# Queries by seven products in a third pass, with their exponentials kept in memory

## The chip, the cores and the metric

The kernel runs on one core of one Trainium2 chip. The core has five engines that run side by side, each with its own list of instructions: TensorE (PE; its weight loads are listed as PEld) multiplies matrices and writes to PSUM; VectorE (DVE), ScalarE (ACT) and GpSimd (POOL) work on elements; SyncE (SP) here only issues DMA transfers. The metric is device time in microseconds for one execution, as the median over runs.

## The reference

S is 2048 rows of x, D is 1024, there are H = 32 heads of DH = 32, and the hidden width FF is 3584. All is float32.

```python
xn = _layernorm(x)
q, k, v = split(xn @ wqkv)                       # [32 heads, 2048, 32] each
pq = einsum("bhsd,hdf->bhsf", q, w_phi); pk = einsum("bhsd,hdf->bhsf", k, w_phi)
phi_q = concat([softmax(pq), softmax(-pq)])      # the same for phi_k
kv = einsum("bhsf,bhsd->bhfd", phi_k, v);  z = einsum("bhsf->bhf", phi_k)
o = einsum("bhqf,bhfd->bhqd", phi_q, kv) / (einsum("bhqf,bhf->bhq", phi_q, z) + 1e-6)
s = o.reshape(S, D) @ wo
g = silu((silu(xn @ w1) * (xn @ w3)) @ w2)
out = x + s * g
```

So there are two branches on the same normalised x: linear attention with a feature map of two softmaxes per head, and a gated feed-forward network. The output joins them.

## The kernel before

**Numbers.** Every large product is made of float32r matmuls. An operand is split into a rounded high part and a low rest (`split`, L89: a copy on ScalarE and a subtraction on VectorE), and a product of two operands takes three matmuls, high by high, high by low and low by high (`PASSES`, L87).

**Seven products.** Most of the large products use a seven-product scheme for 2x2 blocks in place of eight: two tiles of 128 rows form a pair (`pairs`, L66), each operand has seven combinations of its four blocks (`ANAMES`, `BNAMES`, in the order of `ORDER`, L60), and the seven products accumulate in three PSUM banks, from which the four output blocks are read at given points. A pair costs 7 x 12 = 84 matmuls of 128x512 where the plain form costs 96 for the same two outputs of 512 columns.

**Stages, in order.**

1. The start: x is loaded, normalised and transposed; w_phi is folded into the key and query weights (`fold`, L243), so that pk and pq come directly from xn. Transposed x is also written to memory (`store_x`, L223, tensor `xn_d`).
2. Feed-forward products with w1 and w3 (loop at L545), in two halves `tb` of 28 steps `f`, each of seven products: 196 "side steps" per half. Beside them run side tasks at steps given by hand (`at`, `room`, `store_quad`, L383 to L408): the x operands of the second half (`side_x`), weight folds (`side_fold`), the seven combinations of the key and value weights for two passes (`side_kv`, eight units), in the second half those of w2 (`side_w2`) and the splits of query and output weights (`side_split`). Their results go to memory (`wkv_d`, `wqo_d`, `wo_d`, `w2_d`). `room` spreads the splits by an allowance of VectorE time per step. In this stage the instructions of all engines, SyncE too, are in the order of the program text (`in_order`, L46).
3. Keys and values (loop at L763): two passes `c`, each over eight pairs. Each pass has its own seven weight operands of 2 MB in slots `big0` to `big6` and two spare slots (`HOMES`, L148); the next pass's operands are fetched into slots as they come free in the last pair (`fetch`, L157). The x operands of each pair are loaded again (`reload`, L535). In a pair (`heads`, L649) the key half goes through `features` (L104: largest and smallest per head, two differences, exponential, sum) and `scaled`, and small products `kv` (L639) add phi_k by v into one bank `pkv`. `kv_out` (L694) writes the sums with sixteen small stores, for the first pass in the first pair of the second, and for the second pass in step r = 1 of the next stage (L924).
4. The feed-forward product with w2 (loop at L901): seven blocks `kb` times eight pairs, again by seven products, summed over kb in SBUF tiles `acc`. The hidden values are loaded (`hr`) and split per step. In the last kb, `gate` (L819) applies silu to finished sums and stores them (`g_d`), query weights are loaded into the freed tiles, and the queries of tile 0 are computed.
5. The last stage (loop at L1005): for each of sixteen tiles of 128 rows the queries are projected by plain products (`project_q`, L868: 24 matmuls for each of two halves `c` of 512 columns), `queries` (L838) makes the exponentials and scales them, `attend` (L973) transposes them and multiplies by the key/value sums `kvu`, and `finish` (L993) projects by wo (another 48 matmuls), multiplies by the gate, adds x and stores.

Outside the parts that are in program order, the order of each engine's instructions comes from a planner that estimates when each could run. Tiles come from pools with a fixed number of buffers per tag; a new tile waits for the release of an old one.

In `queries` the sum with z is folded in: `ez` is the exponentials times `zb` (the key sums, the same for every row), made by GpSimd, and VectorE's sums of e and ez give one factor per head and sign:

```python
nc.gpsimd.tensor_mul(ez, ef, zb[c])
nc.vector.tensor_reduce(sums[:, 0]..., e3, axis=AX.X, op=OP.add)
...
nc.vector.tensor_mul(e3, e3, by...to_broadcast([P, H, DH]))
```

## Time and profile before

| | |
|---|---|
| median of 3 runs | 2473.88 us (2471.05 to 2474.21) |
| the profiled execution | 2476.03 us, span 2474.2 us |
| TensorE busy | 2408.9 us, 97% |
| VectorE busy | 1718.2 us, 69% |
| ScalarE busy | 896.9 us, 36% |
| GpSimd busy | 668.5 us, 27% |
| DMA | 521.02 MB, mean 211 GB/s |

In the profiled execution stage 3 begins at about 1180 us, stage 4 at about 1514, and the last stage at about 2068. In a row of the profile, "L100 PE MATMUL pm<-wq,xh" is line 100 of the kernel, the engine, the operation, and the tiles written and read by their names; after "x" stands the count, then the busy time and the mean duration of one in nanoseconds, then the engine's idle time before these instructions and what ended it. A row of the timeline begins with its start and its duration. SPq is SyncE's queue of DMA issues.

### The profile page before, as it was taken

The page shows a single profiled execution, that of the slowest core. Times are in us where ns is not written, and L with a number is a line of the kernel's source. Part 1 is how long each engine was busy: PE and PEld are TensorE (multiplying, and loading weights), DVE is VectorE, ACT ScalarE, POOL GpSimd, SP SyncE. Part 2 cuts the span into 40 slices and gives each one's busy share as a digit, 9 for nine tenths or more (in the row PEclk, how much of TensorE's full clock was granted, in tenths as well). Part 3 has the DMA queues.
Part 4 walks back from the last instruction along what each step waited for, and adds up shares of the span by engine and source line. Part 5 has one row for each costly group of instructions (what it writes and reads, how often), then busy time and mean ns, then how long its engine had stood idle before and what let it go on. Part 6 is the DMA issues. An engine that isn't in the chain of part 4 may idle for free.

```text
span 2474.2 us, 35921 instructions
## 1 busy us (share of the span) xinstructions
PE 2408.9 (97%) x13648; PEld 1969.3 (80%) x13648; DVE 1718.2 (69%) x2573; ACT 896.9 (36%) x1555; POOL 668.5 (27%) x481
## 2 busy tenths in 40 slices
PE   5999999999999999999999999999999999999999
PEld 4788878888778888888788788788888887777777
DVE  8667678774477777774566655587888877777775
ACT  6544544443345454443111113422222243222221
POOL 1233445443344545541000000011111112232222
PEclk9999999999999999999999999999999999999999
DMA  8667788875877777766967763623444376322222
GB/s 294 206 218 229 251 275 307 289 261 178 261 276 273 273 264 267 259 227 253 356 213 294 268 209 123 224 98 145 179 170 179 108 275 232 96 73 90 78 85 69
DMA packets 300812, 521.02 MB, mean 211 GB/s; under 512 B 24544, under 2 KB 172000, under 8 KB 298848
## 3 DMA queue, kind: packets, MB, share of 16 engines
q1 hardware_dynamic: 300640, 518.74, 61.1%
q8 instruction: 107, 1.75, 0.3%
q14 instruction: 65, 0.53, 0.1%
HBM read 331.22 MB, written 187.44 MB: 210 GB/s over the span
## 4 chain that ended last, share of the span: by engine, by line
PE 81%; DMA 8%; DVE 5%; issue 2%; ACT 2%; SPq 1%; POOL 1%; ACTq 0%; DVEq 0%; POOLq 0%
PE bankb L575 18%; PE pm L100 14%; PE bankb L882 12%; PE bankc L575 8%; PE bankb L659 7%; PE bankc L882 6%; PE banka L575 4%; PE bankc L659 3%; PE banka L882 3%; PE banka L659 2%; DVE bo L92 1%; PE po L986 1%; PE pkv L644 1%; DMA wkv_d1T<-wkvo 1%; PE pt L980 1%
## 5 line engine op out<-in xcount | busy, mean ns | idle before, releaser
L92 DVE TENSOR_TENSOR bo<-rw,bo 128x512 fp32r<-128x512 f32 x336 | 292.6, 872 | 129.8 <-ACT bo L91 126.3
L91 ACT CAST bo<-rw 128x512 fp32r<-128x512 f32 x336 | 206.4, 622 | 69.8 <-DMA w_d5T<-w2o 8.7
L882 PE MATMUL bankb<-bo,as 128*128 128x512 f32 x816 | 202.3, 391 | 5.2 <-DVE acc L894 5.2
L892 POOL TENSOR_TENSOR acc<-acc,u 128x512 f32<-128x512 f32 x48 | 62.7, 1307 | 483.4 <-ACT u L891 383.0
L270 POOL TENSOR_TENSOR rw<-rw,t 128x512 f32<-128x512 f32 x56 | 79.2, 1414 | 404.5 <-DVE bo L92 404.4
L100 PE MATMUL pm<-wq,xh 128*128 128x512 f32 x768 | 185.3, 394 | 0.0
L882 PEld LDWEIGHTS bankb<-bo,as 128*128 128x128 f32 x816 | 153.9, 189 | 37.7 <-DVE acc L894 5.7
L575 PE MATMUL bankb<-op0A,bo 128*128 128x512 f32 x672 | 160.3, 392 | 8.1 <-ACT bo L91 4.5
L575 PE MATMUL bankb<-op1A,bo 128*128 128x512 f32 x672 | 159.8, 394 | 7.7 <-DVE u L603 4.6
L100 PEld LDWEIGHTS pm<-wq,xh 128*128 128x128 f32 x768 | 142.0, 188 | 31.4 <-issue 2.8
L575 PE MATMUL bankb<-op0S,bo 128*128 128x512 f32 x672 | 163.7, 392 | 2.3 <-ACT h L588 1.3
L575 PE MATMUL bankc<-op0S,bo 128*128 128x512 f32 x672 | 164.3, 393 | 1.2 <-ACT u L601 1.2
L575 PE MATMUL bankb<-op1S,bo 128*128 128x512 f32 x672 | 161.7, 389 | 2.2 <-ACT u L594 2.2
L575 PE MATMUL bankc<-op1S,bo 128*128 128x512 f32 x672 | 161.7, 389 | 0.8 <-issue 0.8
L575 PEld LDWEIGHTS bankb<-op1A,bo 128*128 128x128 f32 x672 | 126.6, 189 | 37.3 <-DVE u L603 7.5
L575 PEld LDWEIGHTS bankb<-op0A,bo 128*128 128x128 f32 x672 | 125.3, 188 | 37.6 <-DVE u L603 5.9
L575 PEld LDWEIGHTS bankb<-op1S,bo 128*128 128x128 f32 x672 | 126.0, 188 | 29.0 <-ACT u L594 2.9
L575 PEld LDWEIGHTS bankc<-op0S,bo 128*128 128x128 f32 x672 | 126.5, 189 | 28.0 <-ACT u L601 1.6
L575 PEld LDWEIGHTS bankc<-op1S,bo 128*128 128x128 f32 x672 | 126.0, 188 | 27.6 <-issue 1.2
L575 PEld LDWEIGHTS bankb<-op0S,bo 128*128 128x128 f32 x672 | 124.8, 188 | 28.7 <-ACT u L594 1.9
L882 PE MATMUL bankc<-bo,as 128*128 128x512 f32 x576 | 147.2, 391 | 0.0
L100 PE MATMUL pm<-wos,oT 128*128 128x512 f32 x576 | 136.3, 390 | 0.0
(201 smaller groups left out, 4679.9 us busy)
## 6 DMA issues: line engine op xcount, KB each, us to landing
rw<-in_w SPq DMA_DIRECT2D x112, 512.0 KB, 5.2
h_d<-h SPq DMA_DIRECT2D x112, 256.0 KB, 7.0
hr<-h_d SPq DMA_DIRECT2D x56, 512.0 KB, 3.5
xoS<-xo_d0S SPq DMA_DIRECT2D x32, 512.0 KB, 9.8
xoS<-xo_d1S SPq DMA_DIRECT2D x32, 512.0 KB, 3.9
room<-in_w SPq DMA_DIRECT2D x56, 256.0 KB, 6.4
xoA<-xo_d0A SPq DMA_DIRECT2D x24, 512.0 KB, 9.4
xoA<-xo_d1A SPq DMA_DIRECT2D x24, 512.0 KB, 4.0
```

The lines of the kernel that those rows point to most:

```text
L91: nc.scalar.copy(hi, src)
L92: (by or nc.vector).tensor_sub(lo, src, hi.bitcast(F))
L100: nc.tensor.matmul(p, xT[dch][:, a], w(dch, b), start=n == 0, stop=n == 3 * ND - 1)
L270: nc.gpsimd.tensor_sub(b11, b22, t2)
L575: nc.tensor.matmul(bank[b], bo[bn][:, w, k], ao[an][:, u, k], start=first and n == 0, stop=LAST[b] == an and n == 11, skip_group_check=True)
L644: nc.tensor.matmul(pkv[sl, m], e[:, m // 4, (m % 4) * P + 32 * h:(m % 4) * P + 32 * h + 32], v[:, 4 * (m % 4) + h], start=first and m == 0 ...
L659: nc.tensor.matmul(bank[b], xo[an][:, u, k], wb[bn][:, w, k], start=an in ("A11", "A12", "S1") and n == 0, stop=LAST[b] == an and n == 11, ...
L882: nc.tensor.matmul(bank[b], t[:, u, pos + k], bos[kb, bn, k][:, w], start=first and n == 0, stop=LAST[b] == an and n == 5, skip_group_chec ...
L892: nc.gpsimd.tensor_add(c, c, u)
L980: nc.tensor.transpose(pt[:, g, :], e[:, (4 * q + g) * P:(4 * q + g + 1) * P], ident)
L986: nc.tensor.matmul(po[32 * g:32 * g + 32, hh, q * P:(q + 1) * P], kvu[sl, G * c + 4 * q + g], et[sl, g], start=True, stop=True, skip_group ...
```

## The change

The queries move from the last stage into stage 3 as a third pass, with c = 2, over the eight pairs, by seven products like the keys. The loop around the seven products is now a function of its own, `seven`, used by `heads` and by the new `queries`. The query weights are no longer split and stored as `wqo_d`; three side units more (`side_kv` with c = 2, one of four in the first half, three in the second) make their seven combinations. The third pass makes the exponentials (`spikes`) and stores them (`e_d`); the last stage loads them (`load_e`), makes the sums and scales (`scales`, for both halves at once, one of the two scalings on GpSimd), two tiles ahead of their use. The transposed x is not stored any more. The splits of wo move from the second feed-forward half into the first two passes of stage 3. The sixteen stores of the second pass's key/value sums move from stage 4 into the first pair of the third pass. In the last stage `attend` of tile i + 1 is cut into parts that stand between groups of twelve matmuls of tile i's output projection. `kvu` is loaded earlier. Side tasks get new steps (folds every 6 in place of 14, key/value units every 11 in place of 12, the units of the second half every 9.5).

```diff
-    HOMES = [(4, 5, 6, 0, 1, 3, 2), (7, 8, 4, 5, 6, 0, 1), (2, 3, 7, 8, 4, 5, 6), (0, 1, 2, 3, 4, 5, 6)]
+    HOMES = [(4, 5, 6, 0, 1, 3, 2), (7, 8, 4, 5, 6, 0, 1), (2, 3, 7, 8, 4, 5, 6), (0, 1, 2, 3, 7, 8, 4),
+             (5, 6, 0, 1, 2, 3, 4)]
...
+    def spikes(t, c, p, e):
+        mm = small.tile([P, 2, 16], F, name="mm2")
+        p3 = p.rearrange("p (h f) -> p h f", f=DH)
+        nc.vector.tensor_reduce(mm[:, 0, :], p3, axis=AX.X, op=OP.max)
+        nc.vector.tensor_reduce(mm[:, 1, :], p3, axis=AX.X, op=OP.min)
+        e4 = e.rearrange("p (h s f) -> p h s f", s=2, f=DH)
+        nc.vector.tensor_sub(e4[:, :, 0], p3, mm[:, 0, :].unsqueeze(2).to_broadcast([P, 16, DH]))
+        nc.vector.tensor_sub(e4[:, :, 1], mm[:, 1, :].unsqueeze(2).to_broadcast([P, 16, DH]), p3)
+        nc.scalar.activation(e, e, AF.Exp)
+        nc.sync.dma_start(e_d[t][c], e)
+
+    def queries(i, xo, wb, steps, pend):
+        t0, t1 = pairs[i]
+        for an, pb in seven(xo, wb):
+            if an == "A11":
+                k0 = work.tile([P, 512], F, name="k0", tag="w")
+                nc.scalar.copy(k0, pb)
+            elif an == "A12":
+                nc.vector.tensor_add(k0, pb, k0)
+                e01 = rwp.tile([P, 2, 1024], F, name="eq", tag="rw")
+                spikes(t0, 0, k0, e01[:, 0])
+            elif an == "S2":
+                d0 = work.tile([P, 512], F, name="d0", tag="w")
+                nc.scalar.copy(d0, pb)
+            elif an == "S1":
+                if pend:
+                    kv(*pend)
+                    kv_out(1, pkv)
+                d1 = work.tile([P, 512], F, name="d1", tag="w")
+                nc.scalar.copy(d1, pb)
+            elif an == "S3":
+                nc.vector.tensor_add(d1, pb, d1)
+                spikes(t1, 1, d1, e01[:, 1])
+            elif an == "S4":
+                nc.vector.tensor_add(d0, pb, d0)
+                e10 = rwp.tile([P, 2, 1024], F, name="eq", tag="rw")
+                spikes(t0, 1, d0, e10[:, 0])
+            else:
+                spikes(t1, 0, pb, e10[:, 1])
+            next(steps)
+        return None
...
-    for c in range(2):
+    for c in range(3):
...
+                    if c < 2:
+                        split_wo(c, i, j)
...
+                    if end and c < 2:
+                        if j < 4 or (j == 4 and c == 0):
+                            wbn.update(fetch(c + 3, j + 2))
+                        if j == 6 and c == 1:
+                            wbn.update(fetch(c + 3, 6))
...
-            pend = heads(i, xo, wb, steps(), pend)
+            pend = (queries if c == 2 else heads)(i, xo, wb, steps(), pend)
...
+    def scales(e):
+        sums = small.tile([P, 2, 2, 16, 2], F, name="sums")
+        for c in range(2):
+            ez = accp.tile([P, 1024], F, name="ez", tag="accE", bufs=3)
+            nc.gpsimd.tensor_mul(ez, e[c], zb[c])
+            nc.vector.tensor_reduce(sums[:, 0, c]..., e[c]..., axis=AX.X, op=OP.add)
+            nc.vector.tensor_reduce(sums[:, 1, c]..., ez..., axis=AX.X, op=OP.add)
+        ...
+        for c, eng in enumerate((nc.vector, nc.gpsimd)):
+            e3 = e[c].rearrange("p (h f) -> p h f", f=DH)
+            eng.tensor_mul(e3, e3, by[:, c]...to_broadcast([P, H, DH]))
+        return e
...
-            kv(*pend)
-            kv_out(1, pkv)
             late_rw += [rwp.tile([P, 2, 2, 512], R, name="late", tag="rw") for _ in range(2)]
...
+    for oT in halves(es[0]):
+        pass
+    for i in range(NT):
+        out_i = output(i, oT)
+        if i + 3 < NT:
+            es[i + 3] = load_e(i + 3)
+        if i + 2 < NT:
+            scales(es[i + 2])
         if i + 1 < NT:
-            xT = split_q(xf)
-        e1 = queries(p, 1)
-        finish(pend[0], oT)
-        pend = (i, e0, e1)
+            for oT in halves(es[i + 1]):
+                next(out_i)
+        for _ in out_i:
+            pass
```

`halves` runs `attend` for both halves of a tile in four parts; `output` is the former `finish`, which now stops after every twelve matmuls to let the next part in.

238 lines of the change are left out of this document (106 added, 132 removed).

## The prediction

> **What bounds the kernel now.** I read the page's busy shares and its chain first, then the chain in order of time and TensorE's instructions at the places where the change cuts, then the stages' busy times, the queue of SyncE, and the DMA answers for the key and value stage.
>
> ```profile
> span 2474.2 us, 35921 instructions
> PE 2408.9 (97%) x13648; PEld 1969.3 (80%) x13648; DVE 1718.2 (69%) x2573; ACT 896.9 (36%) x1555; POOL 668.5 (27%) x481
> PE 81%; DMA 8%; DVE 5%; issue 2%; ACT 2%; SPq 1%; POOL 1%; ACTq 0%; DVEq 0%; POOLq 0%
> ```
>
> TensorE is busy for 97% of the span and carries 81% of the chain. A busy TensorE need not be TensorE at its rate, so the next rows give the rate.
>
> ```profile
> 2041.09 5.60 PE L100 MATMUL pm<-wq,xh 128*128 128x512 f32 x24
> 2046.53 1.52 PE L882 MATMUL bankc<-bo,as 128*128 128x512 f32 x6
> ```
>
> The 24 matmuls of one query projection begin at 2041.09 and the next work begins at 2046.53: 5.44 us, or 0.2267 us each.
>
> ```profile
> 1409.69 2.94 PE bankb L659 x12
> 1430.57 2.94 PE bankb L659 x12
> 2310.99 20.43 PE pm L100 x89
> 2336.64 20.43 PE pm L100 x89
> ```
>
> In the chain in order of time, a pair of key/value tiles takes 1430.57 - 1409.69 = 20.88 us: 84 matmuls are 84 x 0.2267 = 19.04, the rest is the small products of `kv`. A tile of the last stage takes 2336.64 - 2310.99 = 25.65 us: 96 large matmuls are 21.77, and 3.88 are left for `attend`. In the chain both repeat evenly on TensorE alone, so its own work sets their length. Stage by stage (busy us of each engine; clock, DMA share and GB/s last):
>
> ```profile
> 20.00:40.00 20.00, 16.52 (x112) 14.29 (x110) 19.07 (x45) 14.07 (x29) 2.59 (x2) 1.00 0.83 265
> 1540.00:1560.00 20.00, 14.76 (x55) 11.52 (x54) 7.30 (x16) 6.86 (x14) 0.00 (x0) 0.83 0.74 237
> 2040.00:2084.00 44.00, 41.54 (x249) 33.56 (x247) 30.69 (x54) 20.11 (x22) 8.49 (x4) 1.00 0.80 285
> ```
>
> TensorE's idle microseconds gather at the start and at seams such as 1540-1560 and 2040-2084; the rest is dense.
>
> **1. The query product itself.** Removed: 16 tiles x 2 halves x 24 = 768 large matmuls. Added: 8 pairs x 7 products x 12 = 672. The difference is 96, and the trace shows the rate: 96 x 0.2267 = **-21.8 us**. The bounds are narrow, because the added matmuls have the shape and the loop of the two existing passes (19.04 per pair). The new pass so costs 8 x 19.04 = 152.3 us and the last stage falls to 25.65 - 48 x 0.2267 = 14.77 us a tile. This holds as far as the other engines keep up in both places.
>
> **2. VectorE and ScalarE in the new pass.** Per pair there are four `spikes` and three additions, with the durations of the same operations today:
>
> ```profile
> L844 DVE TENSOR_REDUCE mm<-pm 128x16 f32<-128x512 f32 x32 | 22.0, 688 | 35.3 <-PE pm L100 35.3
> L894 DVE TENSOR_TENSOR acc<-bankb,acc 128x512 f32<-128x512 f32 x152 | 104.3, 686 | 24.9 <-PE bankb L882 18.8 <-ACT as L91 2.0
> L850 ACT ACTIVATE e<-e 128x1024 f32<-128x1024 f32 x32 | 34.0, 1062 | 105.0 <-DVE e L847 105.0
> L855 DVE TENSOR_REDUCE sums<-e 128x32 f32<-128x1024 f32 x32 | 39.0, 1219 | 24.0 <-ACT e L850 24.0
> L851 POOL TENSOR_TENSOR ez<-e,zb 128x1024 f32<-128x1024 f32 x32 | 76.7, 2395 | 219.7 <-issue 133.4 <-ACT e L850 86.3
> L1001 POOL TENSOR_TENSOR gx<-gx 128x512 f32<-128x512 f32 x30 | 38.9, 1298 | 71.1 <-issue 37.5 <-DVE rho L858 29.3 <-DVE gx L1000 4.4
> ```
>
> VectorE: four passes over the bank each (two reductions, two differences, all at about the 0.688 of the first row), 16 x 0.688 + 3 x 0.686 = 13.1 us; ScalarE, four exponentials of 1.062 and three copies, about 6. Both lie under the 19.04 of TensorE: nothing. The exponential buffers are two, and the first of a pair is written again one pair later: its second store is issued about 5 us after the fifth product, and 10.9 us lie between that product and the next write, so the store may take 6 us to land. If it is late, VectorE waits, with 6 us to spare.
>
> **3. DMA in the new pass.** Per pair: seven reloaded operands of 512 KB (3.67 MB), four stores of exponentials (2.10 MB), and in pairs 1 to 4 two blocks of w2 operands (1.05 MB), 6.82 MB at most. At 19.04 us that asks for 358 GB/s.
>
> ```profile
> DMA packets 669, 8.49 MB, mean 425 GB/s; under 512 B 70, under 2 KB 70, under 8 KB 177
> 1380.00:1400.00 20.00, 20.00 (x166) 16.13 (x168) 12.85 (x18) 3.66 (x5) 0.21 (x2) 1.00 0.95 368
> ```
>
> The first line is the DMA answer for 1340 to 1360, where the operands of the second pass are fetched: 425 GB/s held for 20 us. The second row gives 368 GB/s at a share of 0.95, with TensorE busy for all of its 20 us. The demand is 84% of that, so I take no cost for the steady pass. The Trainium skill, "DMA: Bandwidth & Descriptors", section "Where 436 GB/s comes from", says that for transfers between HBM and SBUF the HBM side binds at about 358 GB/s; by it pairs 1 to 4 would have nothing to spare, and what is carried over from the seam would lengthen the pass by about 5 us, an estimate worked out below. This trace does not agree: it shows 425.
>
> **4. The new seam between pass two and pass three.** Five operands of 2 MB are fetched as their slots come free, and the sixteen tiny stores of the key/value sums follow on the same queue. Today's seam between pass one and two shows both:
>
> ```profile
> 1346.04 3.01 PE L659 MATMUL bankb<-op3B,xoA 128*128 128x512 f32 x12
> ...
> 1361.26 0.32 SPq L704 DMA_DIRECT2D kv_d<-kva  x1
> ...
> 1375.07 0.81 SPq L540 DMA_DIRECT2D xoA<-xo_d0A  x2
> xoS<-xo_d0S SPq DMA_DIRECT2D x4, 512.0 KB, 18.3
> 1388.74 1.43 PE L659 MATMUL bankb<-op3B,xoA 128*128 128x512 f32 x5
> ```
>
> SyncE spends 13 us or more on the sixteen stores, and only at 1375.07 are the operands loaded for the pair that begins at 1388.74. The four loads of the fifth line, issued in the thick of it, took 18.3 us to land; a load at half of that had about 4 us to spare. In pass three two pairs and one `kv` last 38.8 us, not the 42.7 from 1346.04 to 1388.74, so the spare time is about zero, and four stores of exponentials stand in the same queue. From below, nothing; from above, one late burst, 18.3 less the 13.7 us from 1375.07 to 1388.74, about 5. I take **+2**.
>
> The seam between pass one and two gets its operands earlier (slots 7 and 8 are used too) but shares DMA with the splitting of wo: 0.79 MB a pair beside 3.67, and one subtraction and one copy of 128x512 a pair, 0.7 us each at most on engines that have 6 us to spare. Nothing.
>
> **5. The seam into the second feed-forward stage.** The last `kv` and its sixteen stores leave step 1 of that stage.
>
> ```profile
> 1529.09 0.32 SPq L704 DMA_DIRECT2D kv_d<-kva  x1
> ...
> 1541.79 0.38 SPq L736 DMA_DIRECT2D hr<-h_d  x1
> ...
> 1550.69 0.43 DVE L741 TENSOR_TENSOR sm<-hr 128x256 f32<-128x256 f32 x1 [11.44 <-DMA hr<-h_d]
> 1551.77 2.93 PE L882 MATMUL bankb<-bo,as 128*128 128x512 f32 x6 [5.24 <-DVE acc L894]
> ```
>
> The stores hold SyncE from 1529.09, the load of `hr` goes out only at 1541.79, VectorE waits 11.44 us for it, and TensorE 5.24 us for VectorE. The clock then falls (0.83 over 1540 to 1560): 55 matmuls in 20 us are 12.5 us of work, 7.5 lost. With the stores gone the whole 7.5 can come back; what is late next are the last pair's four stores of exponentials, of which the last follows its product by 4 x 0.688 + 1.062 = 3.8 us, or about 5 with the queue, and stands before the next `hr`. From 0 to -7.5; the removed queue is 12.7 us, the new hold 5, so I take **-6**.
>
> **6. The last stage.** Per tile VectorE keeps four sums and one scaling of 128x1024 at 1.219 each, six small steps of 0.17 to 0.25 (half as many as now, on twice the heads; I take 1.2 together), and the two splits and two products that today's tile has, at the 0.686 of L894: 6.1 + 1.2 + 2.74 = 10.0 us. GpSimd takes over one scaling. No GpSimd operation with a repeated factor is in the trace; the nearest row is the 2.395 of L851, and the other end twice that. So 3 x 2.395 + 2 x 1.298 = 9.8 us, at most 12.2. Both are under 14.77. But the two disturb each other:
>
> ```profile
> 2274.07 1.31 POOL L1001 TENSOR_TENSOR gx<-gx 128x512 f32<-128x512 f32 x1 [2.09 <-DVE rho L858]
> 2274.26 1.15 DVE L862 TENSOR_TENSOR rho<-rho,sums 128x16 f32<-128x16 f32 x1
> ...
> 2289.64 0.17 DVE L862 TENSOR_TENSOR rho<-rho,sums 128x16 f32<-128x16 f32 x1
> ```
>
> The same small step takes 0.17 us alone and 1.15 when it starts under a GpSimd addition, ending with it. VectorE has five operations with two operands in SBUF per tile, and GpSimd will be busy for two thirds of it, so a blocked wait is 5 x 0.66 x half of 2.4 = 4 us if they fall at random: 14.0 of 14.77, still under. Tiles are scaled two ahead, so a short wait harms nobody. For waits that do reach TensorE I take **+2**, between 0 and the case C below. The Trainium skill, "SBUF — State Buffer", section "Who interferes with whom", has the rule behind such a row: a VectorE operation with two SBUF inputs and a GpSimd operation exclude each other for a whole instruction. The trace agrees (0.17 against 1.15). By it the port is taken for at most 9.8 + 2 us of 14.77.
>
> At the head of this stage the first tile's `attend` has no projection to hide under any more. Today 2.46 us are idle between 2040 and 2084, most of it for `kvu`, which is now fetched earlier; after the change TensorE stands, but for the transposes, behind two gates of about 1.06 (as L850, the same shape on ScalarE), two copies of about half of that, and one split (as much again and 0.69): 3 to 4 us. **+1**, between -2 and +3. The end (last product, two VectorE steps, last store) stays.
>
> **7. The start.** The stores of the normalised x leave SyncE.
>
> ```profile
> 37.70 4.93 DMA xn_d<-xf
> ...
> 42.66 0.69 DVE L232 TENSOR_TENSOR xf<-xf 128x512 f32<-128x512 f32 x1 [1.01 <-DMA xn_d<-xf]
> ```
>
> One of them is in the chain, because x is then overwritten in place, but VectorE waits only 1.01 us for it and is itself busy for 19.07 of 20 us there: **-1**, between 0 and -4.9. In the first feed-forward half, ten splits of query weights go and seven of the new operands come; in the second, 22 splits go and 21 come, and the memory moved is nearly the same: nothing.
>
> Sum: -21.8 + 2 - 6 + 2 + 1 - 1 = **-23.8 us**. The profiled execution took 2476.03 us (span 2474.2), 2.15 above the median of the runs; against that median of 2473.88 the forecast is 2450.
>
> **The rivals.** *A*, the sum: 2450, with its own range 2442 to 2458 from the ends of steps 4 to 7. *B*, the third pass is fed too slowly: if SyncE's queue is held by stores that wait for exponentials, or the rate is only the 368 GB/s of the row above, every fetch after the seam is late. The pass moves 8 x 5.77 + 4 x 1.05 = 50.4 MB and carries about 6 MB over from the seam (5 x 2.10 + 3.67 + 0.79 asked for in the last pair, less 20.88 us at 425 GB/s); at 368 GB/s that is 153.3 us, 1 more than TensorE's 152.3. With the seam at its upper end (3 more) and step 5 without gain (6 more) the time is 2460. Against it speaks the 425 GB/s row. By the limit that the Trainium skill states ("DMA: Bandwidth & Descriptors", the section named in step 3) the 56.4 MB would take 157.5 us, and B would be 2464.
>
> *C*, on the other side: in the last stage the chain from GpSimd's products to VectorE's sums, to the scaling on GpSimd, becomes the beat. It decides where a tile takes more than 14.77 + 23.8/16 = 16.3 us. VectorE's 10.0 plus a wait for all of GpSimd's 9.8 would be 19.8; with the scaling on GpSimd at double price (12.2) and three fifths of it waited for, a tile takes 17.3, which is 16 x 2.5 = 40 us more: 2490. For it speaks the 1.15 row; against it, that VectorE's operations with two operands in SBUF are about 2 of its 10 us. At 15.5 a tile it would eat only half of the gain. *D*, all seams at their good ends: -21.8 - 7.5 - 2 - 1 = -32.3, so 2441. That the change does not do what it says isn't to be seen: the matmul counts are in the loops.
>
> **How the numbers follow.** A 0.58, B 0.12, C 0.16, D 0.14. A change under 0.2%, 5 us, is about what cannot be told from none here. Faster takes A and D, half of B and a fifth of C: 0.81. Same takes a sixth of B and a quarter of C, 0.06; slower the rest of both, 0.13 (a B that is worse than its price included). The range reaches from D's value to halfway between B and no change, 2440 to 2470; beyond it I leave 0.05 below and 0.15 above.
>
> **What would show it.** Right: 8 pairs of about 19.0 us after the second pass with no DMA wait above 2 us; tiles of 14.5 to 15 us in the last stage; no 5 us wait of TensorE at the start of the second feed-forward stage. Wrong: TensorE waiting for `xo` or third-pass operands, VectorE idle for `ez` while a bank waits for it, tiles above 16 us, or TensorE idle for over 6 us at the head of the last stage.

## The result, and the profile after

The changed kernel takes 2485.15 us (median of 4 runs, 2483.98 to 2485.47) where the kernel before takes 2472.47 beside it (4 runs, 2470.83 to 2474.21). The ratio is 1.005 (95% interval 1.0033 to 1.0068): it is slower by half a per cent, and not faster by one as forecast. The page of the kernel after begins:

```profile
span 2483.1 us, 35840 instructions
PE 2388.2 (96%) x13552; PEld 1950.1 (79%) x13552; DVE 1704.0 (69%) x2465; ACT 900.8 (36%) x1564; POOL 735.4 (30%) x513
```

TensorE has the 96 matmuls less that the change was to save (13552 for 13648), and 20.7 us less of busy time, yet the span has grown by 8.9 us. What came in is idle time. To see where, the span is cut where each stage's matmuls begin (one matmul of the second feed-forward stage stands 9 us ahead of its cut in the kernel after, among the last products of the third pass). These are rows of TensorE's timeline (start, duration), first of the kernel before, then of the kernel after:

```profile
1175.63 2.66 PE L659 MATMUL bankb<-op2B,xoA 128*128 128x512 f32 x11
...
1514.01 1.65 PE L882 MATMUL bankb<-bo,af 128*128 128x512 f32 x6
...
2067.72 5.61 PE L100 MATMUL pm<-wq,xh 128*128 128x512 f32 x24
```

```profile
1184.05 2.20 PE L639 MATMUL bankb<-op2B,xoA 128*128 128x512 f32 x9
...
1523.07 3.00 PE L639 MATMUL bankb<-op4B,xoA 128*128 128x512 f32 x12
...
1686.34 1.30 PE L913 MATMUL bankb<-bo,af 128*128 128x512 f32 x5
...
2233.32 1.53 PE L1002 MATMUL pt<-ident,e 128*128 128x128 f32 x12 [0.79 <-DVE acc L925]
```

| stretch | before, us | after, us | change | forecast |
|---|---|---|---|---|
| to the first pass | 1175.6 | 1184.1 | +8.4 | -1 |
| first and second pass | 338.4 | 339.0 | +0.6 | 0 |
| third pass | - | 163.3 | +163.3 | +154.3 (152.3 + 2) |
| second feed-forward stage | 553.7 | 547.0 | -6.7 | -16.9 (-10.9 of query matmuls, -6) |
| last stage, to the span's end | 406.5 | 249.8 | -156.7 | -160.2 (-163.2 of query matmuls, +2, +1) |
| sum | 2474.2 | 2483.1 | +8.9 | -23.8 |

The miss of 32.7 us has four places: 9.4 ahead of the first pass, 9.6 in the passes, 10.2 in the second feed-forward stage and 3.5 in the last one. Each has its own view. (The first pass of the same code begins up to 5 us apart from profile to profile, as said below, so the first of the four is the least certain.)

**Ahead of the first pass.** Rows of ScalarE's, VectorE's and TensorE's timelines, in order of time; the bracket tells how long the engine was idle before, and what ended it:

```profile
1083.35 0.62 ACT L90 CAST w2o<-room 128x512 fp32r<-128x512 f32 x1 [3.04 <-DMA w_d6B<-w2o]
1084.00 1.32 DVE L91 TENSOR_TENSOR w2o<-room,w2o 128x512 fp32r<-128x512 f32 x1 [2.87 <-ACT w2o L90]
1085.24 0.68 DVE L584 TENSOR_TENSOR u<-bankb,u 128x512 f32<-128x512 f32 x1
1085.98 5.76 PE L556 MATMUL bankb<-op1A,bo 128*128 128x512 f32 x24 [1.37 <-DVE u L584]
```

A split (`store_quad`) waits 3.04 us until an earlier block's store has left its buffer; VectorE's half of the split waits with it; the addition that frees a bank stands behind in VectorE's queue; TensorE waits 1.37 us for that bank.

**The seam between the second and the third pass.** SyncE's issues, and the first matmul of the third pair:

```profile
1542.15 0.32 SPq L735 DMA_DIRECT2D kv_d<-kva  x1
...
1557.86 0.30 SPq L736 DMA_DIRECT2D z_d<-zs  x1
...
1561.83 1.18 SPq L521 DMA_DIRECT2D xoA<-xo_d0A  x2
...
1569.65 4.64 PE L639 MATMUL bankb<-op4B,xoA 128*128 128x512 f32 x12 [6.61 <-DMA xoA<-xo_d0A]
```

The sixteen small stores take 16 us of the queue (the first seven 1.2 us each, most of the others about 0.5), the reloads for the third pair are issued after them, and TensorE waits 6.61 us for the first one. By stretches of 10 us (busy time of each engine; clock, DMA share and GB/s last):

```profile
1530.00:1540.00 10.00, 10.00 (x106) 8.11 (x105) 4.33 (x10) 2.51 (x4) 0.00 (x0) 1.00 1.00 422
1540.00:1550.00 10.00, 9.57 (x43) 7.62 (x42) 7.09 (x12) 3.67 (x4) 0.00 (x0) 1.00 0.89 339
1550.00:1560.00 10.00, 10.00 (x46) 8.29 (x45) 3.49 (x6) 1.17 (x2) 0.00 (x0) 1.00 0.15 23
1560.00:1570.00 10.00, 3.40 (x15) 2.57 (x14) 4.60 (x8) 2.11 (x2) 0.00 (x0) 0.82 1.03 251
```

DMA falls from 422 to 23 GB/s while the stores go out: from 1550 to 1560 the DMA engines are busy for a share of 0.15 only, with no large transfer issued between 1540.93 and 1558.85. Around the wait the granted clock is 0.82.

**The end of the second feed-forward stage.** TensorE's timeline, and GpSimd's first product with `zb`:

```profile
2200.12 2.73 POOL L884 TENSOR_TENSOR ez<-e,zb 128x1024 f32<-128x1024 f32 x1 [7.47 <-ACT acc L866]
...
2216.02 1.65 PE L913 MATMUL bankc<-late,as 128*128 128x512 f32 x6 [2.93 <-DVE acc L925]
...
2225.12 1.66 PE L913 MATMUL bankb<-late,as 128*128 128x512 f32 x6 [1.87 <-DVE acc L925]
```

```profile
2210.00:2220.00 10.00, 6.05 (x24) 4.35 (x24) 10.00 (x10) 1.53 (x2) 8.61 (x4) 1.00 0.75 254
2220.00:2233.00 13.00, 7.99 (x30) 5.32 (x30) 12.87 (x18) 3.18 (x3) 3.83 (x3) 1.00 0.77 291
```

VectorE is busy for 22.87 of 23 us: the scaling of the first two tiles stands between the additions that free TensorE's banks. Before, 48 query matmuls filled this stretch. Some of the 22.87 us is blocking inside VectorE's operations, as the same small step shows, first under a GpSimd product (2212.97 to 2215.32), then beside none:

```profile
2213.61 1.75 DVE L896 TENSOR_TENSOR by<-by,rho 128x32 f32<-128x32 f32 x1
...
2226.91 0.18 DVE L896 TENSOR_TENSOR by<-by,rho 128x32 f32<-128x32 f32 x1
```

Five operations of the scalings in this stretch (1.81, 1.75, 0.62, 2.55 and 2.61 us) take 9.3 us together; undisturbed, at 0.18 for each of the three small steps and 1.22 for each of the two scalings, they would take 3.0. So about 6 us of the stretch is of this kind, an estimate from these rows.

**The last stage.** A tile takes 15.25 us in the middle. GpSimd's timeline over one tile, and TensorE's longest wait of the stage:

```profile
2329.32 2.38 POOL L884 TENSOR_TENSOR ez<-e,zb 128x1024 f32<-128x1024 f32 x1
2333.64 1.29 POOL L1027 TENSOR_TENSOR gx<-gx 128x512 f32<-128x512 f32 x1 [1.93 <-DVE gx L1026]
2334.88 2.41 POOL L884 TENSOR_TENSOR ez<-e,zb 128x1024 f32<-128x1024 f32 x1
2339.43 1.29 POOL L1027 TENSOR_TENSOR gx<-gx 128x512 f32<-128x512 f32 x1 [2.14 <-DVE gx L1026]
2341.77 2.86 POOL L899 TENSOR_TENSOR e<-e,by 128x1024 f32<-128x1024 f32 x1 [1.06 <-DVE by L896]
2344.60 2.38 POOL L884 TENSOR_TENSOR ez<-e,zb 128x1024 f32<-128x1024 f32 x1
```

```profile
2283.52 1.11 PE L1011 MATMUL po<-et,kvu 64*32 64x128 f32 x32 [6.92 <-DVE oT L91]
```

GpSimd is idle three times per tile, each time for VectorE (1.93 + 2.14 + 1.06 = 5.1 us), and VectorE for GpSimd's `ez` in between (2.43 and 1.55 us ahead of its sums of `ez`). Neither is full; the hand-overs make a ring of 15.25 us. Ahead of the wait of 6.92 us, two small steps of the scaling (0.18 us elsewhere) took 1.90 and 2.26 us under GpSimd's products and stood before the split that TensorE waited for.

### The profile page after: what moved, and what is told of

It is laid out like the page before. It is cut to its first block, busy times and chain, and to the rows that moved or that the text cites. A ratio compares the mean times of both kernels' runs of the same rounds, so it can differ in the third digit from the quotient of the medians.

```text
span 2483.1 us, 35840 instructions
## 1 busy us (share of the span) xinstructions
PE 2388.2 (96%) x13552; PEld 1950.1 (79%) x13552; DVE 1704.0 (69%) x2465; ACT 900.8 (36%) x1564; POOL 735.4 (30%) x513
## 3 DMA queue, kind: packets, MB, share of 16 engines
q8 instruction: 107, 1.75, 0.3%
## 5 line engine op out<-in xcount | busy, mean ns | idle before, releaser
L99 PE MATMUL pm<-wos,oT 128*128 128x512 f32 x768 | 192.1, 400 | 0.0
L99 PEld LDWEIGHTS pm<-wos,oT 128*128 128x128 f32 x768 | 140.3, 189 | 33.1 <-issue 6.3
L556 PE MATMUL bankc<-op0S,bo 128*128 128x512 f32 x672 | 163.3, 391 | 2.2 <-ACT u L582 1.4
L556 PE MATMUL bankb<-op0S,bo 128*128 128x512 f32 x672 | 163.3, 392 | 2.2 <-ACT u L575 2.2
L556 PEld LDWEIGHTS bankb<-op1A,bo 128*128 128x128 f32 x672 | 126.3, 189 | 44.2 <-DVE u L584 14.3
L913 PEld LDWEIGHTS bankc<-bo,as 128*128 128x128 f32 x576 | 107.9, 188 | 24.6 <-DMA bo<-w_d0B 2.0
```

The source lines that it names most:

```text
L99: nc.tensor.matmul(p, xT[dch][:, a], w(dch, b), start=n == 0, stop=n == 3 * ND - 1)
L556: nc.tensor.matmul(bank[b], bo[bn][:, w, k], ao[an][:, u, k], start=first and n == 0, stop=LAST[b] == an and n == 11, skip_group_check=True)
L913: nc.tensor.matmul(bank[b], t[:, u, pos + k], bos[kb, bn, k][:, w], start=first and n == 0, stop=LAST[b] == an and n == 5, skip_group_chec ...
```

## The experiments

All edits are to the kernel after, but for one. Stage lengths are taken at the same cuts as above. Where the stage's code is the same as in the kernel after, the first pass began between 1179.8 and 1185.0 us in eleven profiles, with 553.3 to 556.2 us for the second half of the first feed-forward stage; the second and third pass together took 330.8 to 336.9 us in eight, the third alone 160.6 to 163.7; the second feed-forward stage took 546.5 to 548.2 in eight: less than that is no difference here.

**1. Small stores spread over the next products.**

```diff
-                    kv_out(1, pkv)
+                    kv_out(1, pkv, "h1", late_out)
...
+                    if c == 2 and i and late_out:
+                        nc.sync.dma_start(*late_out.pop(0))
...
```

> The sixteen small stores of the key/value sums, issued in one block inside the first pair of the third pass, are issued one behind each product of the pairs that follow. Theory Q (order of SyncE's queue): the reload of the second pair's operands stood behind the stores, and the DMA engines were nearly idle meanwhile (39 and 14 GB/s in 1548 to 1558); now the reload goes out some 15 us earlier, the wait of 6.61 us for xoA vanishes with the slow clock behind it, and the third pass takes 153 to 156 us instead of 163.3, the whole kernel about 2476. Rival M (memory): the 14 MB asked for around the seam are what is late, so the wait moves or stays, and the pass takes 160 us or more, with the DMA share at 1.0 throughout.

Measured: 2480.83 us, ratio to before 1.0033 (1.0022 to 1.0045). The wait of 6.61 us is gone, another of 1.56 stands a pair later, and the third pass takes 156.0 us, within theory Q's range and 4.6 us under the lowest of the eight profiles above. The second pass, which the edit does not touch, took 172.0 here for 168.4 (168.4 to 172.3 in seven of the eight, 175.7 in one), so both together took 328.0 for 331.7. The whole is 4 us below the kernel after, 2485.15, with overlapping intervals. The empty stretch is gone (410 and 419 GB/s from 1540 to 1560), but where the spread stores run among the large transfers the DMA engines move 217 GB/s at a share of 0.86 (1570 to 1580) and 196 at 1.07 (1590 to 1600). That is a first sign of a second cost, which 13 takes up.

**2. Both scalings on VectorE.**

```diff
-        for c, eng in enumerate((nc.vector, nc.gpsimd)):
+        for c, eng in enumerate((nc.vector, nc.vector)):
```

> In the scaling of a tile both halves are scaled by VectorE, none by GpSimd. Theory L (the two engines exclude each other): GpSimd's work per tile falls from about 10.2 to 7.4 us, VectorE's own scaling no longer collides, VectorE's load rises by about 1.2 to some 11.2 us of 14.3; the tiles in the middle take 14.3 to 14.6 us instead of 15.25, the last stage 234 to 238 us instead of 245.3, the whole kernel about 2477. Rival V (VectorE's load is what counts): the tiles stay at 15.2 us or grow to 15.5 and more, and the last stage takes 246 us or more.

Measured: 2486.31 us, ratio 1.0054 (1.0035 to 1.0073); the last stage takes 251.6 us for 249.8. Most tiles fell to 14.3 to 14.6 us, but four took 16.6 to 20.7, with waits of up to 3.3 us for `oT`. Theory L fell, and so did the hope that less work on GpSimd is enough.

**3. No scaling of the first two tiles at the end of the second feed-forward stage.**

```diff
             if i == 5:
-                scales(es[0])
                 es[1] = load_e(1)
             if i == 7:
-                scales(es[1])
                 es[2] = load_e(2)
```

> The scaling of the first two tiles, which stands in the last two steps of the second feed-forward stage, is left out (the first two tiles of the output so lack their scaling). Theory P (the scaling has lost its cover: 48 query products stood there before): the second feed-forward stage takes 535 to 539 us instead of 547.0, and TensorE is busy for over 9.5 of the 10 us of 25 to 15 us before its end. Rival W (what costs there are the gates' stores, the loads of wo and of the exponentials): the stage stays at 545 us or more.

Measured: 2475.54 us (one run); the second feed-forward stage takes 537.5 us for 547.0. In the stretch 2210 to 2220 of its profile:

```profile
2210.00:2220.00 10.00, 9.81 (x44) 7.78 (x43) 6.74 (x11) 3.66 (x4) 4.15 (x2) 1.00 0.92 342
```

TensorE is busy for 9.81 us, not 6.05. Theory P holds: these scalings, with all that they ask of VectorE and GpSimd, cost 9.5 us there.

**4. Three of the units left out of the second feed-forward half.**

```diff
-    for k in range(1, 4):
-        units.insert(3 * k, (side_kv, 2, k))
     for m, (unit, a, b) in enumerate(units):
-        unit(a, b, HALF + 5 + 19 * m // 2)
+        unit(a, b, HALF + 7 + 12 * m)
```

> The three units that prepare query operands in the second half of the first feed-forward stage are left out (the first half's query unit is stored in their places, so the queries are not the reference's), and the 18 units of w2 stand 12 steps apart again, as in the kernel before. Theory U (the units' GpSimd sums and their closer spacing cost the 6.4 us of that half): the second half, from the first product at 629 to the first pass, takes 547 to 550 us instead of 555.0. Rival N (the loss comes from elsewhere, from the buffers that wait for stores or from what is left out of the splitting of wo): it takes 553 us or more.

(The w2 units are fourteen, not eighteen as the expectation says.) Measured: 2485.37 us (one run). The second half takes 545.3 us for 555.0, more than theory U asked for; the run does not tell the missing units from the wider spacing of the others. But the first half became 10.6 us longer: there one unit's seven buffers were now each held until four stores had read them. That was not foreseen, and pointed to the buffers.

**5. The last stage in its written order, in pieces.** The scaling becomes a generator of three pieces, which stand between the pieces of the output product; all five engines keep the order of the text. The loads of the gate and of x for a tile's two halves also go out together, ahead of its products.

```diff
-    in_order(ENG.SP)
+    in_order(ENG.PE, ENG.Activation, ENG.DVE, ENG.Pool, ENG.SP)
...
-        if i + 2 < NT:
-            scales(es[i + 2])
+        sc = scaling(es[i + 2]) if i + 2 < NT else iter(())
+        next(sc, None)
         if i + 1 < NT:
             for oT in halves(es[i + 1]):
                 next(out_i)
+                next(sc, None)
...
```

> Last stage alone: the scaling of a tile is cut into three pieces, which stand between the pieces of attend and of the output product, and all five engines keep this written order, so that no piece stands ahead of the split that TensorE waits for. Theory O (the order in VectorE's and GpSimd's queues makes a ring of hand-overs of 15.25 us a tile, and a pile of two tiles' scalings ahead of one split costs 7 us at 2276 to 2283): tiles take 14.3 to 14.5 us throughout, the pile vanishes, and the last stage, from the first transposes to the last product block, takes 218 to 222 us instead of 231.3, the whole kernel about 2474. Rival L (GpSimd and VectorE exclude each other, in whatever order): tiles stay near 15.2 us and the stage at 229 us or more.

Measured: 2470.22 us, ratio 0.999 (0.998 to 0.9999). The last stage takes 235.0 us to the span's end for 249.8, 14.8 less (231.3 in the expectation is to the last block of products; 14.8 off that is 216.5, a little under the range). The stretches of 30 us that hold the long wait and the tile above, first in the kernel after, then here:

```profile
2270.00:2300.00 30.00, 23.08 (x200) 18.12 (x194) 26.31 (x34) 5.00 (x9) 19.08 (x10) 0.89 0.56 176
2330.00:2360.00 30.00, 28.24 (x236) 22.28 (x225) 21.46 (x30) 6.66 (x12) 19.75 (x11) 1.00 0.54 175
```

```profile
2270.00:2300.00 30.00, 30.00 (x264) 23.76 (x263) 21.14 (x32) 7.20 (x14) 21.60 (x12) 1.00 0.52 178
2330.00:2360.00 30.00, 30.00 (x290) 23.62 (x270) 20.52 (x31) 7.25 (x13) 21.60 (x12) 1.00 0.58 187
```

TensorE is busy throughout, with GpSimd no less busy than before, and every full tile takes 14.3 us. In the four later runs with this edit (8, 12, 14, 18) the stage takes 235.0 us too. Theory O holds: the order was the cost, not the load (the earlier loads of gate and x were not tried apart).

**6. VectorE relieved at the end of the second feed-forward stage.**

```diff
+        if t < 2:
+            nc.vector.tensor_reduce(kept[t][:, c], e..., axis=AX.X, op=OP.add)
...
-        elif an == "A11":
+        elif an == "A11" or an == "A22" and kb == NKB - 1 and i >= 3:
...
```

> Second feed-forward stage's end: the scalings stay where they are, but VectorE is relieved there. The plain sums of the first two tiles are formed in the third pass (four reductions of 1.22 us less), and in the last steps the addition of one more product of seven goes by ScalarE and GpSimd (about five additions of 0.69 less). Theory P (VectorE's load there is what TensorE waits for): 4.9 + 3.4 us less of VectorE's work make the second feed-forward stage 539 to 542 us instead of 547.0, and the third pass stays as it is. Rival B (the blocked VectorE operations under GpSimd's products are what costs, and GpSimd gets more work): 545 us or more.

Measured: 2492.22 us (one run); the stage takes 550.9 us for 547.0. Less work on VectorE and more on GpSimd, together, lost 4 us; experiment 8 has the first alone. Theory P in this form fell.

**7. The units' sums apart from the operands' own.**

```diff
-            b_sums(r[0], r[2], r[3], r[4])
+            nc.gpsimd.tensor_sub(r[2], r[3], r[2])
+        t1 = free(s0 + 3)
...
+        at(t1 + 1, lambda: nc.gpsimd.tensor_add(r[4], r[2], r[0]))
...
```

> First feed-forward stage: the two GpSimd sums with which a unit begins (key/value and w2 units alike) no longer stand at the step where they fall, but two steps in which the operands' own GpSimd sums are not, one each. Theory G (runs of four GpSimd sums hold up VectorE's subtractions, 1.77 us instead of 0.68): the second half takes 551 to 553 us instead of 555.0, the first half, to its end at 627.5 to 629, 1 to 2 us less too. Rival Q (what delays the steps is the buffers that wait for their stores): both halves stay within 0.7 us.

Measured: 2486.38 us (one run); first half to 626.7, second 556.9, the first pass at 1183.6. No difference: theory G fell.

**8. Three edits together** (1 in both passes, 5, and the reductions of 6).

```diff
-                        kv_out(0, pkv)
+                        kv_out(0, pkv, "h1", late_out)
...
+                    if i and late_out:
+                        nc.sync.dma_start(*late_out.pop(0))
...
```

> Three edits together: the small stores of the key/value sums are spread over the following products in the second and in the third pass, the last stage keeps its written order in pieces, and the plain sums of the first two tiles are formed in the third pass (without the further addition on GpSimd). If each cost was read rightly, they add up: second and third pass together 322 to 325 us instead of 331.7 (waits of about 3 and 6 us gone, and the slow clock behind them), the second feed-forward stage 542 to 545 instead of 547.0, the last stage 15 us shorter; the whole kernel 2458 to 2464, which is faster than both kernels. Rival: what is freed in one place is lost at the next (the reductions moved into the third pass make it longer, the end of the feed-forward stage stays at 547 since GpSimd's part sets it): 2466 or more.

Measured: 2469.57 us, ratio 0.9986 (0.9975 to 0.9996), not more than experiment 5 alone. The last stage kept its gain. The second feed-forward stage took 548.8: moving 4.9 us of reductions away bought nothing. And the passes took 331.4 together, the third one 162.3, with a new wait of 4.8 us for a reload two pairs later: what spreading gained in experiment 1 is lost here. Which of the two additions to the passes does that, the spread in the second pass or the reductions in the third, was not tried apart. The rival held.

**9. Three units without their GpSimd sums.**

```diff
+            t2.append(r[0] if plain else block())
+            if not plain:
+                b_sums(r[0], r[2], r[3], t2[0])
...
```

> The three query units in the second half of the first feed-forward stage keep their loads, copies, subtractions and stores, but form none of their four sums on GpSimd (the operands so hold plain weights, and the queries are not the reference's). Theory G (GpSimd's sums make the units dear: 12 sums of 1.3 us that block VectorE): the second half takes 549 to 552 us instead of 555.0. Rival R (the 21 copies on ScalarE and subtractions on VectorE and their buffers): 554 us or more. Between the two, both.

Measured: 2481.96 us (one run); the second half takes 553.7 us for 555.0, which is inside the spread of the same code. The sums cost nothing that can be seen: what three units and the closer spacing cost (9.7, experiment 4) is then in the splits, their buffers and their stores.

**10. Stores one step sooner in the first feed-forward stage.**

```diff
-            at(step + 2, lambda: nc.sync.dma_start(d, t.bitcast(F)))
+            at(step + 1, lambda: nc.sync.dma_start(d, t.bitcast(F)))
```

> First feed-forward stage: each prepared block is stored one step (2.7 us) after it was split, not two, so its buffer comes free one step sooner. Theory Q (ScalarE waits for a buffer that its store has not left, VectorE's next addition comes late, TensorE waits for its bank): second half 551 to 553 us instead of 555.0, first half, to its end at 627.5 to 629, 1 to 2 us less. Rival N (those waits are not what TensorE's waits hang on): both stay within 0.7 us, or SyncE waits for the split and it gets worse.

Measured: 2470.48 us (one run), 15 us less by one digit, which changes the time of every prepared block's store, and far more than expected. The first half ends at 620.0, the second takes 543.3, and the first pass begins here:

```profile
1163.24 1.98 PE L639 MATMUL bankb<-op2B,xoA 128*128 128x512 f32 x8
```

Waits of TensorE's weight loads for VectorE's addition `u`, in 645 to 1155 (us, times, longest), of the kernel after and here:

```profile
PEld bankb L556 <- DVE u L584: 14.3, 11, 2.2
```

```profile
PEld bankb L556 <- DVE u L584: 2.0, 5, 0.6
```

Theory Q of that stage holds, though its size was far too small: the chain of the rows at 1083 to 1086 is what costs. The listed waits fall by 12.3 us, and the second half by 11.7.

**11. The same digit in the kernel before.**

```diff
-            at(step + 2, lambda: nc.sync.dma_start(d, t.bitcast(F)))
+            at(step + 1, lambda: nc.sync.dma_start(d, t.bitcast(F)))
```

> The kernel before the change, with the same single edit in its first feed-forward stage: every prepared block is stored one step after its split, not two. Theory Q' (both kernels lose time to buffers held by their stores, and the changed one 10 us more, since its units ask for more buffers at a time): the kernel before gains too, but less than the 20.8 us that its first stage-and-a-half gained in the changed one (to 1184.05, then 1163.24): the first pass begins at 1163 to 1166 instead of 1175.63, and the whole takes 2461 to 2464. With the hold gone both kernels would begin the first pass at the same time within 2 us. Rival D (the difference lies in the work itself, GpSimd's 14 operations more): the kernel before gains as much as the changed one and begins the first pass at 1153 to 1157, the whole 2451 to 2455.

Measured: 2459.74 us, ratio 0.9952 (0.9937 to 0.9968).

```profile
1159.39 1.98 PE L659 MATMUL bankb<-op2B,xoA 128*128 128x512 f32 x8
```

The kernel before gains 16.2 us up to the first pass, the changed one 20.8. So most of the hold is old. That the change made it 4.6 us worse is less than the spread of the start of the first pass (1179.8 to 1185.0, and with the sooner stores 1160.4, 1163.0, 1163.2 and 1165.3 in experiments 12, 14, 10 and 18). The second half of the stage is steadier: 553.3 to 556.2 us in the changed kernel for 548.6 in the one before, and with the sooner stores 540.6 to 543.3 in those four runs for 539.9 here. The excess of the changed kernel there falls from some 6 us to some 2, with one profile each of the kernel before. It lies between Q' and D.

**12. Four edits together** (5, 10, the small stores put off to later pairs, and `ez` of the first tile in a buffer that is free a step earlier).

```diff
...
+                    if late_out and i >= 2 * c + 1:
+                        nc.sync.dma_start(*late_out.pop(0))
...
+                scales(es[0], "acc7", 1)
...
```

> Four edits together: stores one step sooner in the first feed-forward stage; the small stores of the key/value sums in the later pairs of the second and third pass, where fewer transfers are asked for; the last stage in its written order in pieces; and the first tile's products with z written into a buffer that comes free one step earlier, so that its scaling begins one step earlier. If the readings hold: 20 us less before the first pass (e10), 15 less in the last stage (e5), 5 to 8 less in the second and third pass together (324 to 327 us instead of 331.7), 0 to 4 less at the end of the second feed-forward stage: 2438 to 2447, faster than both kernels, and than the kernel before with the same sooner stores. Rival: the places trade with each other (the second and third pass, begun earlier, find their operands late): 2450 or more.

Measured: 2461.65 us, ratio 0.9961 (0.9948 to 0.9973). Two gains add up (first pass at 1160.4, last stage 235.0). The two passes take 346.0 us: the small stores cost more in the later pairs, with a wait of 7.8 us in the second pass (not the third, as the expectation of experiment 14 has it), behind the load of a wo block, and one of 12.1 for the first operands of the next stage. The rival held.

**13. Small stores issued by GpSimd.**

```diff
-                nc.sync.dma_start(kv_d[j % 2, s, ...], kva[sl, 4 * s:4 * s + 4])
-                nc.sync.dma_start(z_d[0, c, :, j, s]..., zs[sl, 4 * s:4 * s + 4])
+                nc.gpsimd.dma_start(kv_d[j % 2, s, ...], kva[sl, 4 * s:4 * s + 4])
+                nc.gpsimd.dma_start(z_d[0, c, :, j, s]..., zs[sl, 4 * s:4 * s + 4])
```

> The kernel after, with the 32 small stores of the key/value sums (second and third pass) issued by GpSimd, which has next to nothing to do in the passes, and not by SyncE. Theory Q (each small store holds its queue about 1.2 us, wherever in the passes it stands: 16 to 20 us a pass in which no reload is issued): the waits of 1.5 and 6.61 us for xoA go, no new one takes their place, and the second and third pass together take 322 to 325 us instead of 331.7. Rival M (memory: while small stores run, the DMA engines are busy and move 200 to 290 GB/s, so the reloads come late whoever issues the stores): 328 us or more, with waits for xo of 3 us or more in pairs 2 to 4.

Measured: 2480.5 us, ratio 1.0035 (1.0022 to 1.0048); the second and third pass together 331.6 us, as before. The stretches around the stores:

```profile
1530.00:1540.00 10.00, 9.74 (x104) 7.57 (x103) 4.50 (x9) 2.88 (x4) 3.84 (x7) 1.00 1.18 398
1540.00:1550.00 10.00, 7.68 (x27) 5.89 (x26) 4.37 (x8) 2.60 (x3) 3.85 (x7) 0.83 0.99 199
1550.00:1560.00 10.00, 10.00 (x46) 8.28 (x45) 1.97 (x3) 1.17 (x2) 1.10 (x2) 1.00 0.98 192
1560.00:1570.00 10.00, 6.47 (x25) 4.67 (x25) 8.80 (x15) 3.18 (x3) 0.00 (x0) 0.93 1.02 268
```

SyncE has none of the small stores now, and the DMA engines are busy all the time, but they move half of what they moved before: 199, 192 and 268 GB/s for 415. The stores' own packets are not what fills them: 1.0% of the engines' time over 1500 to 1600, by the DMA answer for that stretch; the large transfers beside them take longer. The reloads come late all the same, by 2.3 and 2.5 us, and VectorE waits 11.5 us in three places for an exponentials' buffer. So the queue's hold is not needed for the loss: theory Q fell as the whole account. M's price holds so far, though its waits of 3 us or more for reloads did not come. In the kernel after, the same loss looks otherwise: there the DMA engines ran nearly empty (0.15 and 23 GB/s). The Trainium skill says in "DMA: Bandwidth & Descriptors", section "Issuing engines are not separate DMA queues", that whichever engine issues them, transfers run interleaved on the same sixteen DMA engines. This run agrees in that the change of issuer bought nothing (331.6 us by GpSimd, 331.7 by SyncE).

**14. Four edits together, with 13 in place of the later stores** (5, 10, 13, and the earlier `ez`).

```diff
...
+            at(step + 1, lambda: nc.sync.dma_start(d, t.bitcast(F)))
...
+                nc.gpsimd.dma_start(kv_d[j % 2, s, ...], kva[sl, 4 * s:4 * s + 4])
...
+                next(sc, None)
...
+                scales(es[0], "acc7", 1)
...
```

> As the four edits together before, but with the small stores in their old place and issued by GpSimd. What the late stores cost there (a wait of 7.8 us in the third pass and of 12.1 us at the start of the second feed-forward stage) should go: first pass at 1160.4, second and third pass together 322 to 326 us, second feed-forward stage 534 to 538, last stage as in that run; the whole 2433 to 2441 by theory Q. By rival M the passes take 330 us and the whole 2442 to 2448. Either is faster than the kernel before and than the kernel before with sooner stores (2459.7).

Measured: 2451.67 us, ratio 0.9908 (0.9893 to 0.9924), faster than the kernel before, and than the kernel before with its sooner stores (0.9952, 0.9937 to 0.9968). First pass at 1163.0, last stage 235.0; the second and third pass take 333.8 and the second feed-forward stage 546.9, neither repaired. In the third pass VectorE waits 13.7 us for an exponentials' buffer that its store has not left, and TensorE 6.9 us for VectorE. The first `ez` did begin 4.5 us earlier before the stage's end; it bought nothing.

**15. Small stores put off to the second feed-forward stage, first attempt.** They are issued by GpSimd, five to a step.

```diff
...
         parts = first
+        for _ in range(5 if r else 0):
+            if late_out:
+                nc.gpsimd.dma_start(*late_out.pop(0))
```

> The kernel after, with all 32 small stores of the key/value sums put off to the first steps of the second feed-forward stage, where the DMA engines move 157 to 245 GB/s, and issued there by GpSimd, which has nothing to do. Theory M (the small stores load the DMA engines: while they ran on another queue, the engines were fully busy at 192 to 268 GB/s for 30 us, some 5 MB less than at 420): without them the reloads of the second and third pass come in time, waits for xo under 1.5 us, the two passes together 321 to 325 us instead of 331.7; the second feed-forward stage takes at most 3 us more. Rival E (what loads memory in the third pass are the exponentials' stores and the carried-over reloads alone): 328 us or more.

Measured: 2482.39 us, ratio 1.0036 (1.0025 to 1.0048), passes 335.4. The edit did not do what it says: GpSimd's queue still has its first store of each pass at 1368.19 and 1536.63, since the planner issues it as soon as its data is there. The run tells nothing on M or E.

**16. The w2 operands later, the small stores in place.**

```diff
-                        if c == 2 and 0 < i < 5:
-                            load_b(0, i - 1)
+                        if c == 2 and 2 < i < 7:
+                            load_b(0, i - 3)
```

> The kernel after, with the eight w2 operands of the third pass (4.2 MB) fetched in pairs 3 to 6 instead of 1 to 4; the small stores stay where they were. Theory M: the pass asks for 303 instead of 358 GB/s in pairs 1 and 2, but the first wait, at the start of pair 2, comes from stores that stand before any of this: it stays at 4 us or more, and only later waits could fall; both passes together 328 to 332 us. Rival E (the demand of pairs 1 to 4 as a whole is too high): the wait at pair 2 falls under 3 us, both passes 326 us or less.

Measured: 2483.53 us (one run). The wait at the third pair is still 5.5 us, both passes take 333.3. So it is not those 4.2 MB. This speaks against E; the small stores are in SyncE's queue here, so it does not tell Q from M.

**17. Small stores held back by their data.** GpSimd first copies the sums into a tile of a pool that only exists once the third pass ends.

```diff
+    def kv_store():
+        t = accp.tile([P, 2, 512], F, name="kvz", tag="accW", bufs=2)
+        for c, (kva, zs) in enumerate(held):
+            nc.gpsimd.tensor_copy(kv, kva)
+            nc.gpsimd.tensor_copy(z, zs)
...
+                    nc.gpsimd.dma_start(kv_d[j % 2, s, ...], kv[sl, 4 * s:4 * s + 4])
...
```

> The kernel after, with the 32 small stores truly in the second feed-forward stage: in the run before, GpSimd's queue still issued them at 1368 and 1536, as early as their data allowed. Here their data is first copied by GpSimd into a buffer that only exists once the third pass ends. Theory M (the small stores load the DMA engines): the DMA rate stays over 350 GB/s from the seam to the third pair, waits for xo are under 1.5 us, the second and third pass together take 321 to 325 us instead of 331.7, and the second feed-forward stage at most 4 us more at its start. Rival E (the exponentials' stores and the carried-over reloads load the memory by themselves): 328 us or more.

Measured: 2486.96 us, ratio 1.0057 (1.0042 to 1.0073). The passes take 321.8 us, the third one 154.0, and TensorE waits for no operand in it. (The sums also wait in another buffer here; so they did in 15, which gained nothing by it.) Without the small stores the same stretches read, and below the dots those where the stores now stand:

```profile
1540.00:1550.00 10.00, 10.00 (x46) 8.29 (x45) 4.62 (x8) 3.42 (x6) 0.00 (x0) 1.00 1.02 415
1550.00:1560.00 10.00, 10.00 (x46) 8.28 (x45) 8.17 (x14) 2.79 (x4) 0.00 (x0) 1.00 1.02 385
...
1680.00:1690.00 10.00, 3.61 (x16) 2.63 (x14) 1.99 (x3) 0.59 (x2) 3.86 (x7) 0.88 1.07 253
1690.00:1700.00 10.00, 9.34 (x33) 7.61 (x34) 1.39 (x2) 1.76 (x3) 4.06 (x8) 0.78 0.91 201
```

```profile
1690.66 4.30 PE L923 MATMUL bankc<-bo,as 128*128 128x512 f32 x10 [7.05 <-DMA bo<-w_d0B]
```

Theory M holds against E: 415 and 385 GB/s with the stores away, 253 and 201 where they now stand, at a share of 1.07 and 0.91. The gain in the passes alone would fit Q as well; it is 13 that speaks against Q, and here the fall of the rate at the stores' new place. And the expectation of at most 4 us more there fell: the second feed-forward stage takes 560.7 us, 13.7 more, 7.05 of it in one wait for a w2 operand. The cost moved with the stores.

**18. All repairs, with 17 in place of 13.**

```diff
...
+        if r == 1:
+            kv_store()
...
```

> All four repairs together, with the small stores truly in the second feed-forward stage. By theory M the passes take 322 to 326 us instead of 333.8 in the run with GpSimd's queue, and the whole 2440 to 2446 instead of 2451.7; by rival E it stays at 2448 to 2455.

Measured: 2452.72 us, ratio 0.9925 (0.9911 to 0.9939), no different from experiment 14: the passes take 322.2, as M had it, but the second feed-forward stage takes 556.7, so that the whole lies in the rival's range. No place was found in these runs where the 32 stores cost nothing; fewer and larger ones were not tried.

## Why the prediction was wrong, by its own steps

**Step 1** held: 96 matmuls are gone, and with the small stores away the third pass takes 154.0 us (experiment 17) where the step had 152.3 for its large products; the last `kv` of the second pass stands in it too.

**Step 2** held for the load, but for its reserve: the third pass's VectorE was to have 6 us to spare on the store of the exponentials. These took 9.4 us to land in the median of 1520 to 1600, and VectorE waited 5.0 us once for such a buffer (0.7 in experiment 17). It is a consequence of step 4.

**Step 3** held: where no small store ran, 385 to 428 GB/s were moved (experiment 17, 1520 to 1560), and the pass had no wait for an operand. (Its 84% are of the 425 GB/s of the first line; of the 368 beside which they stand they would be 97%.)

**Step 4** is the failed term of the passes: +2 forecast for the seam, where the third pass came out 9.0 us longer than forecast. The place was right, and rival B was right on it. So was SyncE's queue as what makes the reload late in this kernel, since the DMA engines run nearly empty meanwhile (0.15, 23 GB/s). The spare time was wrong. The step took 13.7 us from the issue of the late reload to the pair that needs it, from the seam between pass one and two, and set a burst of 18.3 against it. In the kernel after, the reload for the third pair is issued at 1561.83, which is 38.8 us after the pass began, and not 29.0 as at the old seam (1375.07 - 1346.04): the sixteen stores begin 3.9 us later in the pass, and they and the exponentials' stores, which the step named and put no time to, take 5.9 us more. The pair wants it at 1569.65 - 6.61 = 1563.04, 1.2 us after the issue, and it takes 7.8 us: the wait is 6.6. The clock of 0.82 to 0.84 comes on top.

What the step did not have at all shows in experiments 13, 14 and 15. Off SyncE's queue, the same sixteen stores cost as much (third pass 164.5, 166.0 and 167.0 us), as a load on the DMA engines: about 30 us at 192 to 268 GB/s in place of 415, some 30 x (415 - 220) = 5.9 MB not moved (an estimate from the rows of experiments 13 and 17), just where 6 MB are carried over and demand leaves little to catch up with. With the stores out of the passes the third one takes 154.0 and 154.4 us (17, 18). Spread over SyncE's queue they left it at 156.0 once (1), but at 162.3 and 168.2 in two runs with further edits (8, 12). Why large transfers slow down beside small stores, no run shows.

**Step 5** was right on what it priced: the stall at the start of the second feed-forward stage is gone but for 1.2 us. What failed is that a cover was removed without being priced: the 48 query matmuls of the last block had hidden the scaling of the first tile, and two tiles' scalings now stand there with nothing beside them. Experiment 3 gives 9.5 us (one run). That it is VectorE's own load, as the row with 22.87 of 23 us suggests, was not confirmed: 4.9 us less of it bought nothing (8), nor did an earlier start (14). About 6 us of that row are VectorE's operations blocked under GpSimd's products, which step 6 priced for the last stage alone; none of these edits takes them away, and experiment 3 takes them away with all the rest. Which part of the scalings costs is open.

**Step 6**: 14.77 us a tile was right where nothing waits (14.3 measured), and the loads of both engines were right (GpSimd 10.2 by 9.8 forecast). The two were compared with the tile one by one; the ring through both was left to rival C, which priced it at 17.3 us and wanted 16.3. It is 15.25, and beside it one pile of two tiles' scalings ahead of a split costs 6.92. Both come from the order in the queues (5): with the same load and the same products of GpSimd in another order they are gone, and less work on GpSimd did not help (2). That the stage as a whole missed by only 3.5 us is luck, since two errors offset: the order costs 14.8 us for the 3 that were forecast as waits, but without it the stage takes 235.0, 8.3 less than the 406.5 - 163.2 = 243.3 on which the forecast was built.

**Step 7** said "nothing" for the first feed-forward stage, since as many units go as come. That counted the operations. What costs is the time that a buffer is held by its store: of the excess of some 6 us in the second half, some 4 go when the stores are issued sooner (10, 11, 12, 14, 18). The sums on GpSimd are not seen to cost anything (9, 7), and the rest is open. That the changed units suffer more because they ask for more buffers at a time is the likely reason, and was not tried by itself.

The rivals shared one gap: none had a place where removed work had been the cover of other work, and none had buffers.

## What to carry to other kernels

Before a piece of TensorE's work is moved away, list what ran beside it, since that work stays and now costs its full length. Price small strided stores twice: by the time for which they hold the queue that also issues the next operands, and by what the DMA engines move while they run; moving them to another queue, which takes away the first cost alone, did not help here. A spare time that is read at an old seam holds only if what stands ahead of it in the queue starts as early and is as long. Where two engines hand a tile to and fro, add up the ring with the waits that the queues' order puts in. Look at how long a buffer is held by its store before work is taken away.
